# Two models in one kernel: where attention's and the state model's transposes, and the table functions, stand in the instruction order

## The chip, the cores and the metric

One core of a Trainium2 chip runs the whole program. The metric is the device time in microseconds (us) of one execution; lower is better. The engines that matter are TensorE (PE; its weight loads are shown as PEld), VectorE (DVE), ScalarE (ACT), GpSimd (POOL) and SyncE (SP), which issues nearly all transfers. Each engine works its own instructions strictly in the order in which they stand; between engines they wait for each other by semaphores.

## The reference

```python
# A: dilated local attention, x (1, 2048, 448), 16 heads of 28, window of 8 keys, 2 apart
qkv = x @ wqkv                                    # -> q, k, v
logits[s, w] = q[s] . k[s - 2*w] * 28**-0.5       # masked where s - 2*w < 0
o = softmax(logits, over w) @ v[s - 2*w]
a = o @ wo
# B: state model, x (1, 2048, 448), 448 complex states
Lam_bar = exp(dt * Lam);  B_bar = ((Lam_bar - 1) / Lam)[:, None] * Bmat
Bu = x @ B_bar.T
h[t] = Lam_bar * h[t-1] + Bu[t]
y = 2 * real(h @ Cmat.T) + x * Dskip
out = concatenate([a, b], axis=-1)                # (1, 2048, 896)
```

## The kernel before

All data fit in SBUF. For attention, the 2048 positions lie as 128 partitions by 16 slots `j`. The kernel computes, in this order on PE:

- **Transposes of attention's x** (`g_xta(jp)`, line 298): eight transposes by PE for a pair of slots, and one DVE copy of the pair from PSUM to `xTA` (L305). Pairs 7 to 0 hold slots 15 to 0.
- **Projections** (`proj(t, j)`, line 309): four matmuls of a slot with the weights of key (t=1), query (t=0) or value (t=2) (L312), then an ACT copy out of PSUM (L316). Key slots 15 to 6 come first, then queries 15 to 8, keys 5 to 0, values 15 to 0 and queries 7 to 0.
- **State model's preparation**: `b_weights(t)` (L327, seven products of B with the small matrices `G`, copied by ACT into `BT`, L329), and `b_x(j)` (L337, transposes of the state model's x for j = 0 to 7, copied into `xT`, by DVE for even j, L339, by ACT for odd j, L342).
- **The state model**, in two halves of its 448 complex states (four and three groups of 64): `ssm_in(half, j)` for j = 0 to 7 (L372, L378, ACT copy L379), a scan over the 256 chunks (`scan_mul` L387 and L388 on DVE, `scan_pe` L397 and L398 on PE, the scan itself L406 on DVE, `scan_mul` and `scan_pe` again, ACT copy L413), `ssm_mix` (L420, L422), and `ssm_out` (L432, L434, ACT copy L436, one output transfer each). Half 1's `ssm_in` stands on PE behind half 0's first `scan_pe`. The four transposes of C (`c_weights`, L352, DVE copy L354) stand between.
- **Attention's sum over values** (`av`, L537): PE adds up products `attn * v` that DVE makes one by one (`pv_mul`, L520), and `wo_j` (L554) multiplies by `wo`.

Beside this DVE carries the logits: two halves of the slots, four pieces each, every piece being one product of queries and keys (`mul`, L457), two additions (`half` L460, `quarter` L463), and, after every second piece, `rest` (L466, L467, L469); then the softmax (L485 to L496). The first piece needs queries 8 to 15 and keys from slot 6 up; the third and later pieces also need the keys' halo, rows of neighbouring partitions that SP copies from SBUF to SBUF (`halo`, L566, L567).

The order on DVE comes from a small planner at build time. `add(cost, fn)` queues a piece of DVE work with a cost in us. Two running sums are kept, the planned time of PE (`load[0]`) and of DVE (`load[1]`). Each PE step calls `pe(cost)`, which raises the first and calls `pump()`; `pump` writes queued pieces into the program for as long as DVE's sum is below PE's sum plus `lead`. `need` writes out a piece that must now be there. DVE copies of transposes and the state model's own DVE work are written where the main program calls them, so they land between queued pieces.

`tables()` (line 288) is such a piece: three DVE instructions (L289, L291, L292), and it leaves six ACT functions (L294 to L296: sine, absolute value, sine, for two slices) in a list `acts`. `proj` takes one of them out behind every second projection, as soon as the list has any:

```python
        ACT.copy(dst, src)
        count[2] += 1
        if acts and count[2] % 2 == 0:
            acts.pop(0)()
        pe(0.76)
```

All PSUM tiles come from one pool of eight banks.

Of the kernel before, what the change touches and what calls it, by code (L numbers as in the profile page):

```python
# [36 lines left out]
def kernel(  # L37
# [29 lines left out]
    def bank(dt=F32):  # L67
        return psum.tile([128, 512 if dt == F32 else 1024], dt, tag="b", name="b")
# [88 lines left out]
    acts = []  # L157
    count = [0, 0, 0]
    load = [6.0, 6.0]

    def add(cost, fn, ok=None):
        todo.append((cost, fn, ok))
        return todo[-1]

    def pop():
        c, fn, _ = todo.pop(0)
        fn()
        load[1] += c

    def pump(lead=0.0):  # L170
        while todo and load[1] < load[0] + lead and (todo[0][2] is None or todo[0][2]()):
            pop()
# [4 lines left out]

    def pe(cost):
        load[0] += cost
        pump()  # L180

    def dve(cost):
        load[1] = max(load[1], load[0]) + cost
# [115 lines left out]
    def g_xta(jp):  # L299
        tp = bank(BF16)  # L300
        tpv = tp[0:KT].rearrange("p (k j n) -> p k j n", k=4, j=2)
        for kt in range(4):
            for jj in range(2):
                PE.transpose(tpv[:, kt, jj, :], xnA[:, 2 * jp + jj, KT * kt:KT * (kt + 1)], ident[:])  # L304
        V.tensor_copy(xTA[:, :, 2 * jp:2 * jp + 2, :], tpv)  # L305
        dve(0.69)
        load[0] += 0.45

    def proj(t, j):
        ps = bank()  # L310
        for kt in range(4):
            PE.matmul(ps[:, 0:D], xTA[:, kt, j, :], wts[:, t, kt, :], start=(kt == 0), stop=(kt == 3))  # L312
        src = ps[:, 0:D].rearrange("p (h d) -> p d h", h=H)
        dst = (q_s[:, :, j * H:(j + 1) * H] if t == 0 else
               k_s[:, :, HALO + j, :] if t == 1 else v_s[:, HALO + j])
        ACT.copy(dst, src)  # L316
        count[2] += 1
        if acts and count[2] % 2 == 0:
            acts.pop(0)()
        pe(0.76)  # L320


    def b_weights(t):
        ps = bank()
        for kt in range(4):
            for i in range(2):
                PE.matmul(ps[0:KT, 128 * kt:128 * (kt + 1)], Bn[:, t, KT * kt:KT * (kt + 1)], G[:, i, t, :],  # L327
                          start=(kt == 0 and i == 0), stop=(kt == 3 and i == 1))
        ACT.copy(BT[:, :, t, :], ps[0:KT].rearrange("p (k n) -> p k n", k=4))  # L329
        pe(0.45)  # L330

    def b_x(j):
        tp = bank(BF16)
        tpv = tp[0:KT].rearrange("p (k c n) -> p k c n", k=4, c=2)
        for kt in range(4):
            for c in range(2):
                PE.transpose(tpv[:, kt, c, :], xnB[:, c, j, KT * kt:KT * (kt + 1)], ident[:])  # L337
        if j % 2 == 0:
            V.tensor_copy(xT[:, :, j, :], tp[0:KT].rearrange("p (k n) -> p k n", k=4))  # L339
            dve(0.69)  # L340
        else:
            ACT.copy(xT[:, :, j, :], tp[0:KT].rearrange("p (k n) -> p k n", k=4))  # L342
        load[0] += 0.45
# [21 lines left out]
    def ssm_in(hf, j):  # L365
        banks = []
        for pr_ in pairs(halves[hf]):
            ps = bank()
            banks.append(ps)
            for i, t in enumerate(pr_):  # L370
                for kt in range(4):
                    PE.matmul(ps[:, i * NC:(i + 1) * NC], BT[:, kt, t, :], xT[:, kt, j, :],  # L372
                              start=(kt == 0 and i == 0), stop=(kt == 3 and j == 0 and i == len(pr_) - 1))
        for ps, pr_ in zip(banks, pairs(halves[hf])):
            n = len(pr_)
            if j > 0:
                for i, t in enumerate(pr_):
                    PE.matmul(ps[:, i * NC:(i + 1) * NC], R[:, 0, t, :], Z[:, t, j - 1, :], start=False, stop=(i == n - 1))  # L378
            ACT.copy(Z[:, pr_[0]:pr_[0] + n, j, :], ps[:, 0:n * NC].rearrange("p (t c) -> p t c", t=n))  # L379
        pe(0.54 * len(halves[hf]))  # L380
# [192 lines left out]
    add(2.5, params3)  # L573
    has_R = [add(0.5, lambda: build_R(0))]
    has_G = add(1.0, build_G)
    for jp in (6, 5, 4, 3):
        proj(1, 2 * jp + 3)
        proj(1, 2 * jp + 2)
        g_xta(jp)
    proj(1, 7)  # L580
    g_xta(2)
    proj(1, 6)
    has_tab = add(6.2, tables)
    has_D = add(0.6, build_D)
    proj(0, 15)
    g_xta(1)
# [11 lines left out]
    need(has_G)  # L598
    for j in range(15, -1, -1):
        proj(2, j)  # L600
        if j % 2 == 0 and j < 14:
            b_weights(j // 2)
    for k in range(1, T - 1):
        has_R.append(add(0.6, lambda k=k: build_R(k)))
    halo(lambda lo, hi, a_, b_: v_s[lo:hi, a_:b_])
    for j in range(7, -1, -1):
        proj(0, j)
        b_x(j)
    for n_, g in enumerate((0, 1, 2, 3)):
        logits(0, n_, g)  # L610
    sm1, sm0 = softmax(1), softmax(0)
# [94 lines left out]
```

## Time and profile before

| what | value |
|---|---|
| runs shown | 182.07 us median of 3 (181.9 to 185.15) |
| the profiled execution's own time | 184.28 us |
| its span, first to last instruction | 182.5 us |
| mean granted clock of TensorE | 0.972 |
| PE busy | 167.1 us (92%) |
| DVE busy | 146.9 us (80%) |
| ACT busy | 95.2 us (52%) |
| chain that ended last | PE 58%, DVE 32%, ACT 7% |

Times in the views are microseconds from the span's start. Busy time says how long an engine worked on instructions, not that the work was on the chain that sets the end. A line of the waits view names who waited, for whom, the total in us, the number of times and the longest. A line of the timeline gives start, length, engine, source line, operation, operands, and in brackets the idle time ahead of it and what ended that.

### The profile page before, as it was taken

The numbers are of one execution on the slowest core, as the hardware profiler recorded it, in microseconds if no ns is written. First come the engines' busy times: TensorE is split into PE (matmuls) and PEld (weight loads), VectorE is DVE, ScalarE is ACT, GpSimd is POOL, SyncE is SP. The second block draws the span as 40 slices with busy tenths as digits, with TensorE's granted clock in tenths as the row PEclk, the third lists the DMA queues.
The fourth block names the chain that finished last, engine by engine and source line by source line (L and its number), as shares of the span: only waits on it lengthen the run. The fifth ranks groups of instructions, "written<-read, shape, count | busy, mean of one in ns | idle before, by whom it ended". The sixth has DMA issues, their size and how long they took to land.

```text
span 182.5 us, 3794 instructions
## 1 busy us (share of the span) xinstructions
PE 167.1 (92%) x1584; PEld 121.9 (67%) x1586; DVE 146.9 (80%) x179; ACT 95.2 (52%) x184; POOL 2.8 (2%) x22
## 2 busy tenths in 40 slices
PE   6776999999995699999999859999999999999992
PEld 7544655556673478887886525566658988887870
DVE  1674794999999999509999999994999999946721
ACT  2463429999874135442468843447832234426431
POOL 3000000000000000000001000000000000000000
PEclk9999999999999579999999978999999999999999
DMA  6999930187881000000000000211214101011212
GB/s 173 328 243 264 336 81 0 25 189 143 179 165 14 0 0 4 0 4 0 0 4 0 0 0 25 77 52 50 75 58 121 42 27 54 27 54 52 79 50 75
DMA packets 13279, 14.01 MB, mean 77 GB/s; under 512 B 4543, under 2 KB 12495, under 8 KB 13135
## 3 DMA queue, kind: packets, MB, share of 16 engines
q1 hardware_dynamic: 13191, 13.77, 29.2%
q8 instruction: 12, 0.20, 0.5%
q14 instruction: 5, 0.04, 0.1%
q10 hardware_dynamic: 71, 0.01, 0.0%
HBM read 6.89 MB, written 3.67 MB: 58 GB/s over the span
## 4 chain that ended last, share of the span: by engine, by line
PE 58%; DVE 32%; ACT 7%; issue 1%; POOL 0%; DVEq 0%; POOLq 0%; ACTq 0%
PE b L537 16%; PE b L432 12%; DVE u L457 11%; PE b L372 9%; PE b L554 7%; PE b L312 4%; DVE u L460 3%; DVE l L463 2%; DVE u L406 2%; DVE u L305 2%; PE b L135 2%; PE b L434 2%; PE b L378 2%; PE b L304 2%; PE b L422 2%
## 5 line engine op out<-in xcount | busy, mean ns | idle before, releaser
L312 PE MATMUL b<-wbuf,u 112*128 112x448 bf16 x192 | 40.0, 353 | 4.1 <-DVE u L305 3.8
L520 DVE TENSOR_TENSOR k_s<-u,v_s 128x1792 bf16<-128x1792 bf16 (+1 forms) x40 | 33.6, 897 | 4.8 <-PE b L537 4.8
L457 DVE TENSOR_TENSOR u<-q_s,k_s 128x7168 bf16<-128x7168 bf16 x8 | 31.1, 3886 | 2.8 <-ACT q_s L316 2.7
L372 PE MATMUL b<-xT,BT 112*128 112x256 bf16 x224 | 29.7, 290 | 3.9 <-DVE xT L339 3.8
L537 PEld LDWEIGHTS <-k_s 128*112 128x112 bf16 x512 | 30.6, 130 | 2.0
L537 PE MATMUL b<-ident,k_s 128*112 128x128 bf16 x512 | 30.9, 219 | 0.0
L312 PEld LDWEIGHTS <-u 112*128 112x128 bf16 x192 | 17.6, 97 | 18.4 <-DVE u L305 4.4
L372 PEld LDWEIGHTS <-BT 112*128 112x128 bf16 x224 | 23.1, 104 | 8.3 <-DVE xT L339 3.9
L379 ACT CAST u<-b 128x512 bf16<-128x512 f32 (+1 forms) x32 | 15.6, 535 | 23.9 <-PE b L378 15.7
L432 PE MATMUL b<-Cw,u 128*128 128x448 bf16 x112 | 24.9, 364 | 0.0
L559 ACT CAST ya<-b 128x448 bf16<-128x448 f32 x15 | 8.1, 537 | 16.8 <-PE b L554 13.4
L432 PEld LDWEIGHTS <-u 128*128 128x128 bf16 x112 | 10.9, 101 | 8.3 <-issue 1.1
L460 DVE TENSOR_TENSOR u<-u 128x3584 bf16<-128x3584 bf16 x8 | 16.2, 2022 | 0.2
L436 ACT CAST yo<-b 128x448 bf16<-128x448 f32 x16 | 8.6, 537 | 13.4 <-PE b L434 9.9
L554 PE MATMUL b<-u,q_s 112*128 112x448 bf16 x64 | 14.4, 352 | 0.0
L423 ACT CAST u<-b 128x512 bf16<-128x512 f32 (+1 forms) x28 | 13.1, 558 | 1.0 <-PE b L422 1.0
L316 ACT CAST k_s<-b 128x448 bf16<-128x448 f32 x16 | 8.1, 549 | 6.7 <-PE b L312 6.7
L547 ACT CAST q_s<-b 112x512 bf16<-112x512 f32 x14 | 7.3, 596 | 8.1 <-PE b L537 8.0
L305 DVE COPY u<-b 112x1024 bf16<-112x1024 bf16 x8 | 5.5, 690 | 6.6 <-PE b L304 6.6
L316 ACT CAST q_s<-b 128x448 bf16<-128x448 f32 x16 | 8.3, 534 | 3.5 <-PE b L312 3.5
L422 PE MATMUL b<-u,R 128*128 128x255 bf16 x49 | 9.9, 280 | 0.2 <-ACT u L413 0.2
L420 PE MATMUL b<-u,ident 128*128 128x512 bf16 (+1 forms) x28 | 10.1, 360 | 0.0
(119 smaller groups left out, 182.4 us busy)
## 6 DMA issues: line engine op xcount, KB each, us to landing
u<-in_B_x_dram SPq DMA_DIRECT2D x2, 896.0 KB, 14.8
out_dram<-yo SPq DMA_DIRECT2D x16, 112.0 KB, 1.7
out_dram<-ya SPq DMA_DIRECT2D x16, 112.0 KB, 2.3
u<-in_A_x_dram SPq DMA_DIRECT2D x3, 448.0 KB, 5.5
wbuf<-in_A_wqkv_dram SPq DMA_DIRECT2D x3, 392.0 KB
k_s<-k_s SPq DMA_DIRECT2D x1, 784.0 KB
v_s<-v_s SPq DMA_DIRECT2D x1, 784.0 KB, 5.9
k_s<-k_s SPq DMA_DIRECT2D x1, 588.0 KB
```

The costliest lines, as they stand in the source:

```text
L312: PE.matmul(ps[:, 0:D], xTA[:, kt, j, :], wts[:, t, kt, :], start=(kt == 0), stop=(kt == 3))
L316: ACT.copy(dst, src)
L372: PE.matmul(ps[:, i * NC:(i + 1) * NC], BT[:, kt, t, :], xT[:, kt, j, :], start=(kt == 0 and i == 0), stop=(kt == 3 and j == 0 and i == le ...
L379: ACT.copy(Z[:, pr_[0]:pr_[0] + n, j, :], ps[:, 0:n * NC].rearrange("p (t c) -> p t c", t=n))
L422: PE.matmul(ps[:, i * NC + 1:(i + 1) * NC], R[:, j, t, :], Z[:, t, T - 1, 0:NC - 1], start=False, stop=(i == n - 1))
L423: ACT.copy(Z[:, sl, j, :], ps[:, 0:n * NC].rearrange("p (t c) -> p t c", t=n))
L432: PE.matmul(ps[:, 0:D], Z[:, t, j, cols], Cw[:, t, :], start=(t == 0), stop=False)
L457: V.tensor_tensor(pr[:], qv, kv, ALU.mult)
L460: V.tensor_tensor(pr[:, :, 0:14, :], pr[:, :, 0:14, :], pr[:, :, 14:28, :], ALU.add)
L520: V.tensor_tensor(pv_of(i), attn[:, s, H * j0:H * (j0 + nj)].rearrange("p (j h) -> p j h", h=H) .unsqueeze(2).to_broadcast((128, nj, DH, H ...
L537: PE.matmul(acc[kt // kb][0:KT, o:o + 128], pvf[:, jj, KT * kt:KT * (kt + 1)], ident[:], start=(s == 0 and o == 0), stop=(s == W - 1 and o ...
L554: PE.matmul(ps[:, 0:D], oTs[n_ % 3][:, kt, jj, :], wo_p[:, kt, :], start=(kt == 0), stop=(kt == 3))
```

## The change

Five edits, all of them in the order of the work; no instruction is added, removed or resized.

1. Attention's transposes stand two pairs ahead of the projections that read them, not one: pair 6 is transposed before the first key projection, and pair `jp - 2` between the two key projections of pair `jp`.
2. The state model's eight `b_x` move from between queries 7 to 0 to between the value projections, `b_x(0)` behind value 15, `b_x(7)` behind value 1; the `b_weights` steps stand behind the even values (14, 12, ... 2).
3. The six table functions on ACT wait until 18 projections have been written, which is behind query 8, so the first stands behind key 4.
4. `pe` calls `pump(1.0)`: the planner lets DVE's queued pieces run up to 1.0 us ahead of PE's sum.
5. The queued cost of `tables` is 5.2, not 6.2.

```diff
     def pe(cost):
         load[0] += cost
-        pump()
+        pump(1.0)
...
-        if acts and count[2] % 2 == 0:
+        if acts and count[2] > 18 and count[2] % 2 == 0:
             acts.pop(0)()
...
-    for jp in (6, 5, 4, 3):
-        proj(1, 2 * jp + 3)
-        proj(1, 2 * jp + 2)
-        g_xta(jp)
+    g_xta(6)
+    for jp in (7, 6, 5, 4):
+        proj(1, 2 * jp + 1)
+        g_xta(jp - 2)
+        proj(1, 2 * jp)
     proj(1, 7)
-    g_xta(2)
     proj(1, 6)
-    has_tab = add(6.2, tables)
+    has_tab = add(5.2, tables)
...
     for j in range(15, -1, -1):
         proj(2, j)
-        if j % 2 == 0 and j < 14:
-            b_weights(j // 2)
+        if j % 2 == 1:
+            b_x(7 - j // 2)
+        elif j > 0:
+            b_weights(j // 2 - 1)
...
     for j in range(7, -1, -1):
         proj(0, j)
-        b_x(j)
```

In the built program this gives the following order on DVE. The copies of pairs 1 and 0 stand behind the three table instructions; the four `xT` copies stand among the first three logits pieces (before among the third and fourth); and ahead of half 0's first `scan_mul` there stand one `quarter` and one `mul` more than before (`mul`, `half`, `quarter`, `mul` in place of `mul`, `half`). Half 1's scan (L406) no longer has a `mul` between it and the `scan_mul` ahead of it. On SP the order of transfers is the same but for the four loads of `wo`, which stand behind the 13th and not the 14th output transfer of the state model.

## The prediction

> **What bounds it.** First the waits of PE and DVE, since these two hold the chain that ended last.
>
> ```profile
> PE b L312 <- DVE u L305: 3.8, 5, 0.8
> PE b L372 <- DVE xT L339: 3.8, 1, 3.8
> PE b L397 <- DVE wbuf L387: 2.3, 2, 2.1
> DVE u L305 <- PE b L304: 6.6, 5, 2.7
> DVE wbuf L387 <- ACT u L379: 6.4, 1, 6.4
> DVE u L457 <- ACT q_s L316: 2.7, 1, 2.7
> ```
>
> The two take turns. PE waits five times for the copy of a transposed pair, once for the last xT copy, and at the scans; DVE waits for transposes, for late queries, and for half 0 to be done. Then the timeline shows where each wait stands.
>
> ```profile
> 9.38 1.69 PE L312 MATMUL b<-wbuf,u 112*128 112x448 bf16 x8 [0.79 <-DVE u L305]
> ...
> 22.54 12.27 PE L312 MATMUL b<-wbuf,u 112*128 112x448 bf16 x64
> ...
> 30.14 0.96 ACT L316 CAST q_s<-b 128x448 bf16<-128x448 f32 x2
> ...
> 31.14 3.89 DVE L457 TENSOR_TENSOR u<-q_s,k_s 128x7168 bf16<-128x7168 bf16 x1 [2.66 <-ACT q_s L316]
> ...
> 60.90 6.42 PE L372 MATMUL b<-xT,BT 112*128 112x256 bf16 x32 [3.76 <-DVE xT L339]
> ...
> 67.60 1.91 PE L372 MATMUL b<-xT,BT 112*128 112x256 bf16 x16
> ...
> 73.39 2.03 DVE L460 TENSOR_TENSOR u<-u 128x3584 bf16<-128x3584 bf16 x1
> ...
> 81.81 0.69 DVE L387 TENSOR_TENSOR wbuf<-u,tab 128x1024 bf16<-128x1024 bf16 x1 [6.39 <-ACT u L379]
> ...
> 106.47 0.39 PE L397 MATMUL b<-wbuf,ident 128*128 128x512 bf16 x1 [2.08 <-DVE wbuf L387]
> ...
> 108.85 2.53 PE L432 MATMUL b<-Cw,u 128*128 128x448 bf16 x7
> ...
> 111.42 1.49 PE L432 MATMUL b<-Cw,u 128*128 128x448 bf16 x7
> ...
> 138.20 9.10 PE L537 MATMUL b<-ident,k_s 128*112 128x128 bf16 x160
> ```
>
> Query 8 is the sixth of the sixteen projections from 22.54, so PE has it at 22.54 + 6 x 0.767 = 27.1, but ACT evicts it at 30.6 to 31.1, behind table functions of 1.06 and 1.07: that is why the logits start at 31.14. From there DVE has no wait until 75.4. PE meanwhile waits for a DVE copy until 60.90, and its next 32 matmuls take 6.42; later 16 of the same matmuls take 1.75 from their start at 67.60 to that of the step behind them. From 108.85 PE runs without a gap to the end; what sets the time is when it gets there.
>
> **The head (edits 1, 3, 5).** Steps come from starts in the timeline: a projection 0.767 (1.53 for eight matmuls), a pair's transposes 0.46, a DVE copy 0.61, an eviction 0.53, after 0.16 from the last matmul. Pair 6 is transposed by 6.3 (its x is there: the transfer's last packet ends at 5.65), so key 15 starts at 6.5. Pair 5's x lands at 7.65, which costs PE 0.4 once. Then 12 projections up to query 14 (9.2) and six transposes (2.8) bring PE to 6.5 + 0.4 + 9.2 + 2.8 = 18.9, where it was 22.54 before: the 3.8 of waits go. The other loads land earlier than they are used (pairs 3 and 2 9.4, query weights 10.9, pairs 1 and 0 12.6, B's x 24.6). Six queries more end at 23.5, and with ACT free of table functions query 8 is out at 23.5 + 0.16 + 0.53 = 24.2. DVE must also be there. Before, it ended the piece ahead of the logits (L282) at 28.5, with 3.9 of waits for transposes since 5.71 (the list's 6.6 less its first 2.65): 24.6. Laid end to end in the new order I get 23.7. The copies of pairs 1 and 0, now behind the tables, end by 23.2; their first reader, key 3, comes at 25.0. So the logits start at 24.4, 6.7 earlier, DVE and PE about equal.
>
> **Logits up to the first scan (2, 4).** Before, DVE ran from 31.14 to 75.4 without a wait: 44.3. Now a quarter (1.1) and a mul (3.9) more stand ahead of scan_mul: 49.3, so it starts at 24.4 + 49.3 = 73.7. Three waits could break in. The third mul needs the keys' halo: issued when key 2 is out (34.6 before, now 27.5), its last packet ended at 46.9, 12.3 later; now 39.8, against 42.5 when DVE gets to it. The four xT copies need b_x: PE ends keys at 28.1 and works 19.0 for values (16 x 0.767), B products (7 x 0.44) and transposes (8 x 0.45); b_x(4) is ready at 39.1 and DVE wants it at 39.4. ACT in that stretch has 16 x 0.45, 7 x 0.48, 4 x 0.91 and four table functions of 0.75 to 1.05, 17.6 in all; it lags PE by up to 2.5, which the eight banks hold. Without that cover each us of lag delays DVE by as much.
>
> PE: values end at 47.1, queries 7 to 0 at 53.2. xT is complete by 46.8, so ssm_in starts at 53.2 and not 60.90, at full clock: 1.75 + 7 x 2.19 = 17.1 (before 19.8), then C's transposes 1.5 and ssm_in(1, 0) 1.3: 73.1. Here a new wait appears: scan_pe needs scan_mul, done at 74.3 and 74.9. PE is idle about 1.2 and again 0.4, ends scan_pe at 75.55 where it was 84.53: 9.0 ahead. Behind PE's wait stand the other seven ssm_in of half 1 and all that follows, so a late DVE here costs in full.
>
> **The clock.** After the 3.76 wait 32 matmuls cost 6.42 where 32 x 0.109 = 3.5 would do, a loss of 2.9; after 2.08 the first ssm_out took 2.37 from 108.85 to 111.22 where the next takes 1.33; after waits of 0.79 nothing slowed (1.69 for eight). The new wait of 1.2 (1.6 with its second part) lies between; nearer to 0.79, I take no loss, and 1.5 to 2.9 as the other end. The Trainium skill (TensorE: Matmul & The Clock Gate, What's actually happening) has the clock fall only after an idle window of about 3.4 us. The trace differs: it fell after 2.08. By the page the new wait would be safe and the sum unchanged; I don't lean on it.
>
> **The second half.** PE, from 75.55: ssm_in 8.1, scan_pe 0.87, two more ssm_in 3.28, three ssm_mix 2.6, so half 1's first scan_pe could start at 90.4. DVE, from 74.9: C's copies 2.14, scans 2.44, scan_mul 1.3, half 2.05, quarter 1.13, rest 2.33, mul 3.8, so the scan_mul for it starts at 90.1 and ends at 90.6 and 91.1: PE waits 0.3 and 0.25, as before (0.36 and 0.25), and nothing is gained. DVE then scans (1.87) as soon as PE is through, at 91.6 at the latest, instead of doing a mul of 3.9 first; the second scan_mul ends by 94.0 and 94.5, PE wants it after four ssm_mix (3.47) at 95.0: the 2.25 without PE work ahead of 106.47 go. With no pause the clock stays up: 0.6 less around the last scan_pe and ssm_mix, 1.04 less in the first ssm_out. Sum on the chain: 9.0 + 2.25 + 0.6 + 1.04 = 12.9.
>
> **The tail.** The first L537 moves from 138.20 to 125.3. DVE: logits end at 107, softmax maxima at 112.6 (5.6); ACT's exponentials stand one output earlier and are done as DVE asks (before DVE lost 2.24); 7.5 more to 120.1. The first products come 5 us before PE wants them (3.5 before), each 0.96 against PE's 0.89 to 1.27 per step, so PE stays the bound. The loads of wo, behind the 13th output on SP's queue, go out at about 121 (136.39 before), and the first L554 wants them at 147.09 - 12.9 = 134.2; SP carries nothing else that anyone waits for.
>
> Span 182.5 - 12.9 = 169.6. The profiled execution took 184.28, of which 1.8 lie around the span, and is 1.2% above the median; the saved time is the same on both, so the forecast is 182.07 - 12.9 = 169.2.
>
> **Rivals.** (1) Half a head: the logits start late because something else in the head binds, a load or DVE's chain of small parameter instructions (about 40 of 0.16 to 0.2). If only the table functions' delay goes, query 8 is out at 27.1 + 0.7 = 27.8 and DVE free at 28.5: start 28.5, 4.1 later, 173.3. For: DVE and PE are within 0.5 of each other, so neither may slip. Against: each load landed before its new use but one. (2) ACT paces the values: by busy time and not steps it needs 16 x 0.53 + 7 x 0.6 + 4 x 1.01 + 3.9 = 20.6 against 19.0; banks then hold PE back and the xT copies hold DVE: with the lag of 2.5, 1.6 to 4 lost, 170.8 to 173.2. For: b_x(4) has 0.3 of slack. Against: back to back, its steps were 0.42 to 0.48. (3) The halo: transfers from SBUF to SBUF that slow down by other traffic hold the third mul and everything behind it on DVE, xT(6) and scan_mul included. It costs 1:1 from a landing at 42.5 on: no gain is left at 42.5 + 12.9 = 55.4, 2% slower begins at 59, and a halo of 33 in place of 12.3, landing at 60.5, gives 169.2 + 18 = 187.2. For: the third mul began only 0.9 after the landing before, so the halo is the nearest thing to a bound there. Against: keys' and values' halo both took about 12, and the loads from HBM end by 26, before the new start at 27.5.
>
> **Chances.** Forecast 0.70 (167.2 to 172.1: down by the 1.6 that PE waits at 73 and by the 0.4 that pair 5 waits for its x, up by a cooled clock), rivals (1) and (2) 0.23 together, a halo (or another wait) that eats the gain to within 2% 0.04, one that turns it slower 0.03. About 2% is what a measurement of this kernel tells from none. All of the first two cases lie below 178.4. Cooled clock and rival (1) together make more than that; the range takes in the clock and half of (1), 169.2 + 2.9 + 2 = 174, and below it 167.
>
> **What would show it.** The first L457 at about 24.4 with next to no wait for ACT; no wait of L312 for L305 over 0.5; L372 starting at about 53 with no wait for L339 and 16 matmuls in 1.75 from the first; the 6.4 of L387 gone, and a wait of L397 for L387 of 1 to 2 in its place at 73; none of 2 near 95; L432's first seven as quick as the next; L537 at about 125. A first L457 after 27, or DVE idle ahead of an xT copy or the third L457, would prove the forecast wrong at that step.

## The result

| | before | after |
|---|---|---|
| median of four runs | 182.71 us (181.9 to 185.15) | 172.68 us (172.09 to 173.17) |
| the profiled execution, its time and span | 184.28, 182.5 | 172.66, 170.9 |
| mean granted clock of TensorE | 0.972 | 0.998 |

The change makes the kernel faster: ratio 0.946, 95% interval 0.940 to 0.953. The forecast was 169.2 in a range of 167 to 174, so the gain is there and the time is 3.5 above the forecast. The span fell by 11.6; the sum had said 12.9.

The page of the changed kernel, its first line and the clock by fortieths of the span:

```profile
span 170.9 us, 3793 instructions
...
PEclk9999999999999999999999999999999999999999
```

From 6.47, behind the first transposes, the clock is up until 170.3, 0.6 before the end. The waits of PE, then those of DVE ahead of the logits' products (who waits, for whom, total us, times, longest):

```profile
PE b L397 <- DVE wbuf L387: 1.6, 1, 1.6
...
PE b L304 <- DMA u<-in_A_x_dram: 0.9, 1, 0.9
PE b L422 <- ACT u L413: 0.7, 1, 0.7
PE b L398 <- DVE wbuf L388: 0.2, 1, 0.2
```

```profile
DVE u L457 <- ACT tab L294: 0.5, 1, 0.5
...
DVE u L457 <- ACT q_s L316: 0.3, 1, 0.3
```

The 3.8 of L312 for L305 and the 3.8 of L372 for L339 are gone. What is left on PE, beside a wait of 1.4 at the start that was there before, is one new wait at the scan, 1.6, one for a load, 0.9, and small ones. The timeline (start, length, engine, line, operation, and in brackets the wait ahead) shows where the marks of the forecast stand:

```profile
7.11 0.65 PE L304 MATMUL b<-ident,u 128*112 128x128 bf16 x8 [0.88 <-DMA u<-in_A_x_dram]
...
25.18 3.89 DVE L457 TENSOR_TENSOR u<-q_s,k_s 128x7168 bf16<-128x7168 bf16 x1 [0.31 <-ACT q_s L316]
...
33.24 3.89 DVE L457 TENSOR_TENSOR u<-q_s,k_s 128x7168 bf16<-128x7168 bf16 x1 [0.51 <-ACT tab L294]
...
43.63 3.89 DVE L457 TENSOR_TENSOR u<-q_s,k_s 128x7168 bf16<-128x7168 bf16 x1
...
53.87 3.66 PE L372 MATMUL b<-xT,BT 112*128 112x256 bf16 x32
...
75.58 0.38 PE L397 MATMUL b<-wbuf,ident 128*128 128x512 bf16 x1 [1.56 <-DVE wbuf L387]
...
96.12 0.38 PE L397 MATMUL b<-wbuf,ident 128*128 128x512 bf16 x1
...
98.27 1.49 PE L432 MATMUL b<-Cw,u 128*128 128x448 bf16 x7
...
126.58 3.63 PE L537 MATMUL b<-ident,k_s 128*112 128x128 bf16 x62
```

L372's 32 matmuls take 3.66 at once (6.42 before), the second scan has no wait (2.08 before), and the first L432 is as quick as its followers (2.53 and 1.49 before). The chain's steps happened as the sum has them, each 0.7 to 1.3 later than the forecast put it.

### The profile page after: what moved, and what is told of

Same layout as the page of the kernel before. It is cut to its first block, busy times and chain, and to the rows that moved or that the text cites. A ratio compares the mean times of both kernels' runs of the same rounds, so it can differ in the third digit from the quotient of the medians.

```text
span 170.9 us, 3793 instructions
## 1 busy us (share of the span) xinstructions
PE 162.5 (95%) x1584; PEld 120.0 (70%) x1586; DVE 146.7 (86%) x179; ACT 95.7 (56%) x184; POOL 2.8 (2%) x22
## 3 DMA queue, kind: packets, MB, share of 16 engines
HBM read 6.89 MB, written 3.67 MB: 62 GB/s over the span
## 4 chain that ended last, share of the span: by engine, by line
PE 50%; DVE 34%; ACT 6%; issue 4%; DMA 3%; SPq 0%; DVEq 0%; ACTq 0%
PE b L537 17%; PE b L432 12%; DVE u L457 11%; PE b L554 7%; PE b L312 6%; DVE u L460 6%; DVE l L463 3%; DMA u<-in_A_x_dram 3%; PE b L422 2%; PE b L420 2%; DVE R L207 2%; PE b L434 2%; DVE l L466 2%; ACT k_s L316 2%; DVE u L406 1%
## 5 line engine op out<-in xcount | busy, mean ns | idle before, releaser
L312 PE MATMUL b<-wbuf,u 112*128 112x448 bf16 x192 | 40.1, 352 | 0.1
L537 PEld LDWEIGHTS <-k_s 128*112 128x112 bf16 x512 | 30.6, 130 | 2.0
L457 DVE TENSOR_TENSOR u<-q_s,k_s 128x7168 bf16<-128x7168 bf16 x8 | 31.1, 3889 | 0.9 <-ACT tab L294 0.5
L537 PE MATMUL b<-ident,k_s 128*112 128x128 bf16 x512 | 30.9, 219 | 0.0
L312 PEld LDWEIGHTS <-u 112*128 112x128 bf16 x192 | 17.7, 97 | 14.0 <-DVE u L305 0.5
L372 PE MATMUL b<-xT,BT 112*128 112x256 bf16 x224 | 26.9, 272 | 0.1
L372 PEld LDWEIGHTS <-BT 112*128 112x128 bf16 x224 | 21.7, 97 | 3.3
L432 PE MATMUL b<-Cw,u 128*128 128x448 bf16 x112 | 23.8, 352 | 0.0
L432 PEld LDWEIGHTS <-u 128*128 128x128 bf16 x112 | 10.5, 98 | 7.5
L316 ACT CAST v_s<-b 128x448 bf16<-128x448 f32 x16 | 9.2, 612 | 0.8 <-PE b L312 0.8
```

The costliest lines, as they stand in the source:

```text
L432: PE.matmul(ps[:, 0:D], Z[:, t, j, cols], Cw[:, t, :], start=(t == 0), stop=False)
L457: V.tensor_tensor(pr[:], qv, kv, ALU.mult)
L537: PE.matmul(acc[kt // kb][0:KT, o:o + 128], pvf[:, jj, KT * kt:KT * (kt + 1)], ident[:], start=(s == 0 and o == 0), stop=(s == W - 1 and o ...
```

## The experiments

Waits, spans and clocks are of the profiled execution; ratios are to the kernel before on the same chip. A span is 1.8 shorter than the time.

**One edit undone at a time.** First the look-ahead of the transposes (edit 1):

```diff
-    g_xta(6)
-    for jp in (7, 6, 5, 4):
-        proj(1, 2 * jp + 1)
-        g_xta(jp - 2)
-        proj(1, 2 * jp)
+    for jp in (6, 5, 4, 3):
+        proj(1, 2 * jp + 3)
+        proj(1, 2 * jp + 2)
+        g_xta(jp)
     proj(1, 7)
+    g_xta(2)
     proj(1, 6)
```

> The changed kernel with its first edit undone: transposes one pair ahead again, everything else as changed. Theory (the chain runs head, then logits on DVE, then the first scan, then PE to the end, so that each us by which the logits start later costs a us): PE waits again some 0.8 five times for pair copies, less the 0.9 and 0.5 it now waits for loads; query 8 leaves ACT at about 27.8 and DVE is free at 28.5 to 29.1, so the first L457 starts 3.3 to 3.9 later than its 25.2, and the span is 174.2 to 174.8 (time 176 to 176.6). Rival A (DVE has slack later on, the head does not count): span 170.9 to 171.9. Rival B (the look-ahead is worth what PE waited less the load waits, 2.4, at the end): span 173.3.

Measured: 181.74 (180.58 to 183.27), ratio 0.987 (0.978 to 0.996). That is 9.1 above the whole change (172.68) and 5 above the expectation; the profiled execution, the slowest of the four, is 7 above it. The timeline of its head:

```profile
6.82 3.17 PE L312 MATMUL b<-wbuf,u 112*128 112x448 bf16 x8 [0.58 <-DVE u L305]
...
10.80 0.22 DVE L190 TENSOR_TENSOR sn<-sn,rk 128x56 f32<-128x56 f32 x1 [1.87 <-ACT sn L201]
...
12.23 0.69 DVE L305 COPY u<-b 112x1024 bf16<-112x1024 bf16 x1
...
12.98 2.31 PE L312 MATMUL b<-wbuf,u 112*128 112x448 bf16 x8 [2.25 <-DVE u L305]
...
16.93 3.17 PE L312 MATMUL b<-wbuf,u 112*128 112x448 bf16 x8 [0.79 <-DVE u L305]
...
34.30 3.89 DVE L457 TENSOR_TENSOR u<-q_s,k_s 128x7168 bf16<-128x7168 bf16 x1 [0.73 <-ACT q_s L316]
```

Two things I had not priced. The planner's lead of 1.0 (edit 4) writes a parameter piece, which waits for ACT, ahead of the next pair's copy; DVE works in order, so PE's wait for that copy grows to 2.25 (0.8 at most in the kernel with edits 2 and 3 below, which has neither the look-ahead nor the lead). And the clock is at half until 10.48 (until 4.8 to 7.1 in every other profile here) and again from 13.89 to 20.72, behind these waits: the same eight matmuls take 3.17 and not 1.69. The logits start 9.1 later than in the changed kernel. So what edit 4 costs or brings depends on edit 1.

A third thing stands at the scan. PE waits 1.57 for half 0's scan_mul, as it does in the changed kernel (1.56), but here the clock halves behind it, from 85.57 to 88.98:

```profile
84.72 0.38 PE L397 MATMUL b<-wbuf,ident 128*128 128x512 bf16 x1 [1.57 <-DVE wbuf L387]
...
86.33 2.77 PE L372 MATMUL b<-xT,BT 112*128 112x256 bf16 x12 [0.22 <-issue]
```

The same twelve matmuls take 1.47 behind that wait in the changed kernel. So the new wait, which the forecast took to cost no clock as the likelier of its two cases, can cost it.

The table functions (edit 3):

```diff
-        if acts and count[2] > 18 and count[2] % 2 == 0:
+        if acts and count[2] % 2 == 0:
```

> The changed kernel with its third edit undone: the six table functions stand again behind every second projection from the moment the tables are there. Theory (one chain): ACT reaches the first sine behind query 13 and waits for the tables until 23.1, then has two table functions of about 1 and the evictions in turn, so query 8 is out at 26.8, the first L457 starts 1.6 later than its 25.2, and the span is 172.5 (time 174.3); ACT lags behind PE by more, which the eight banks may or may not hold. Rival A (harmless, as other work covers it): span 170.9 to 171.3. Rival B (ACT's lag fills the banks and stops PE in the value stage): span above 174.

Measured: 177.34 (176.99 to 178.05), ratio 0.963 (0.958 to 0.968); 3 us above the expected 174.3, and 4.7 above the whole change. Its timeline:

```profile
22.67 1.06 ACT L294 ACTIVATE tab<-R 128x1024 bf16<-128x1024 f32 x1 [2.89 <-DVE R L292]
...
24.47 1.07 ACT L295 ACTIVATE R<-R 128x1024 f32<-128x1024 f32 x1
...
26.27 1.18 ACT L296 ACTIVATE tab<-R,hpib 128x1024 bf16<-128x1024 f32 x1
27.32 0.98 ACT L316 CAST q_s<-b 128x448 bf16<-128x448 f32 x2
28.33 3.89 DVE L457 TENSOR_TENSOR u<-q_s,k_s 128x7168 bf16<-128x7168 bf16 x1 [3.96 <-ACT q_s L316]
```

Three table functions, not two, stand ahead of query 8, the first of them waiting 2.89 for DVE's preparation with the queries' evictions behind it. DVE waits 3.96 for query 8; the logits start 3.15 later. With them the first scan_mul is late and PE waits long for it, now long enough to cool the clock (half from 78.79 to 82.21):

```profile
PE b L397 <- DVE wbuf L387: 4.5, 1, 4.5
```

The span of 175.2 is in rival B's range, but not for its reason: PE's longest wait for an eviction by ACT is 0.3.

The state model's transposes and B products (edit 2):

```diff
-        if j % 2 == 1:
-            b_x(7 - j // 2)
-        elif j > 0:
-            b_weights(j // 2 - 1)
+        if j % 2 == 0 and j < 14:
+            b_weights(j // 2)
...
         proj(0, j)
+        b_x(j)
```

> The changed kernel with its second edit undone: the state model's transposes of x stand again between queries 7 to 0. Theory (each engine only has to be there in time): with logits 6 us earlier DVE reaches the last xT copy at 53.8, when PE ends the last transposes at 54.5, so the wait of 3.8 ahead of L372 does not come back but one of 0.8 to 1.4, the clock stays up, and the span grows by 0.5 to 1.4 (171.4 to 172.3, time 173.2 to 174.1). Rival (the move itself took the wait of 3.8 and the cooled clock of 2.9 away): 5 to 6.7 more, span 176 to 177.6.

Measured: 171.54 (171.22 to 171.82), ratio 0.931 (0.926 to 0.935), no slower than the whole change; the spans, 169.4 to 170.0, are below the expected 171.4 to 172.3. PE's waits at ssm_in and at the scan:

```profile
PE b L372 <- DVE xT L339: 1.0, 1, 1.0
...
PE b L398 <- DVE wbuf L388: 0.2, 1, 0.2
```

With the logits 6.5 earlier, the last xT copy is only 1.0 late, and it takes the place of the wait of 1.6 at the scan. Edit 2 moves a wait from one place to the other. It also brings the 0.5 that DVE waits at the second L457, which this kernel has not.

The planner (edits 4 and 5, `pump()` and 6.2 again):

> The changed kernel with edits 4 and 5 undone: the planner has no lead and the tables cost 6.2, so DVE's scan_mul of half 0 stands one quarter and one mul earlier and half 1's scan again behind a mul. Theory (DVE's order only moves the wait): no wait of PE for half 0's scan_mul (1.8 gained, scan_pe at 73.9 and not 75.6), DVE idle 2 there, but PE waits about 0.5 for half 1's first scan_mul and about 2.4 for its second one, behind the mul of 3.9; the span is 171.5 with the clock up and 173 where that wait cools it (time 173.3 to 174.8). Rival A (an earlier scan_mul is what counts): span 169.2. Rival B (the lead is worth most of the gain): span above 175.

Measured: 172.84 (171.81 to 173.88), ratio 0.938 (0.930 to 0.946). The wait ahead of the second scan is back:

```profile
PE b L397 <- DVE wbuf L387: 2.3, 2, 2.1
```

and the four executions fall into two groups: spans of 172.1 and 172.0 at a mean clock of 0.99, and 170.1 and 170.0 at 0.998 and 1.0. Both are 1 to 1.5 below what I expected. The timeline of the first, which is the profiled one:

```profile
95.83 0.39 PE L397 MATMUL b<-wbuf,ident 128*128 128x512 bf16 x1 [2.08 <-DVE wbuf L387]
...
98.03 2.82 PE L432 MATMUL b<-Cw,u 128*128 128x448 bf16 x7
...
101.01 1.51 PE L432 MATMUL b<-Cw,u 128*128 128x448 bf16 x7
```

The same wait of 2.08 cooled the clock (half from 97.62 to 101.03, 3.41 long), by the mean clocks in two executions of four. One such stretch lowers the mean clock by 0.01 and costs 2.0 of span where PE is on the chain. Without it edits 4 and 5 bring nothing that shows here.

**One or two edits alone on the kernel before.** Edit 1 alone:

> The kernel before with the first edit alone. Theory (one chain): PE reaches query 8 some 3 earlier, but DVE is done with the tables only at 23.9, and ACT then has three table functions and the evictions ahead of query 8, as in the changed kernel without its third edit (first sine to first L457 5.7 there), so the first L457 starts at 29.6, 1.5 ahead of the kernel before; PE waits longer for the last xT copy (5 in place of 3.8) and the clock cools as before. Span 180.5 to 181.5 (the kernel before: 182.5). Rival (the 3.8 of PE waits for pair copies come off the end): span 178.7.

Measured: 181.22 (180.1 to 183.48), ratio 0.989 (0.977 to 1.000). The logits start at 30.94, hardly earlier than in the kernel before: the late queries' evictions stand behind table functions as before. This profile also has a late load: PE waits 1.96 for pair 6's x, and a stretch at half clock follows (9.31 to 12.73). Two of the four spans, 178.3 and 179.2, are below the expected 180.5 to 181.5 and close to the rival's 178.7, so what edit 1 brings alone is not settled. Edits 1 and 3 together:

> The kernel before with edits 1 and 3, without the moved state-model transposes and without the planner's lead. Theory: the first L457 at 25.0, but DVE then stands ahead of PE at the xT copies and PE again behind them: L372 starts at 57.3 (53.9 in the changed kernel), the wait ahead of it is 2.8 and cools the clock in some runs, and half 1's second scan_mul waits behind a mul, 2.1, which cooled it in half the runs of the kernel without the lead. Span 174.3 with the clock up, 176 to 178 with one or two cooled windows of 2. Rival A (edits 2, 4 and 5 are worth nothing at all, since each alone could be undone for nothing): span 170 to 172. Rival B (edits 2, 4 and 5 hold half the gain): above 178.

Measured: a time of 175.26 in the profiled execution and of 179.09 to 181.31 in the three others, spans of 173.5 (clock 1.0), 177.3, 178.3 (both 0.98) and 179.5 (0.971); the spread is too wide for a ratio, and two of the spans are above the expected 178. The logits start at 25.16. Without edits 2, 4 and 5 two waits of the kernel before are there again, the first of them shorter (2.8 for 3.8):

```profile
PE b L372 <- DVE xT L339: 2.8, 1, 2.8
PE b L397 <- DVE wbuf L387: 2.3, 2, 2.1
```

In the profiled execution neither cooled the clock, and its 173.5 is 9.0 of the 11.6; in the others the mean clocks tell of two or three stretches at half clock, and 4 to 6 of the gain are gone. Edits 2 and 3 together:

> The kernel before with edits 2 and 3, the transposes one pair ahead as before and no lead. Theory: as the head of PE and DVE is that of the kernel before but for ACT, the first L457 starts at 28.5; PE ends its queries at 57.1 and goes on without a wait at full clock, scan_pe at 77.0; 4.0 behind the changed kernel without its lead (170.1 with the clock up): span 174.1, and 176 to 177 with a cooled window or a wait for the first xT copy. Then the changed kernel without its look-ahead (178.8 to 181.5) lost 5 by its first edit's absence together with the lead, not by the absence alone. Rival (the look-ahead by itself is worth 8 to 10): span 179 to 181.

Measured: 177.21 (176.87 to 179.51), ratio 0.972 (0.958 to 0.986), spans 175.1 to 177.7, all at 0.99: the logits start at 28.46, since the head's waits are there,

```profile
PE b L312 <- DVE u L305: 3.8, 5, 0.8
...
PE b L397 <- DVE wbuf L387: 2.3, 2, 2.1
```

and the clock is at half from 100.89 to 104.3 behind the second of these. Three of the four spans (175.1 to 175.6) lie between the two cases of the expectation, 174.1 and 176 to 177 with a cooled clock, and one above. This kernel and the one with edit 1 undone differ in edits 4 and 5 alone: with them, but without the look-ahead, the logits start at 34.30 and not at 28.46, and the median is 181.74 and not 177.21.

**The clock by itself.** The kernel before, with 60 idle matmuls (of the identity with itself, into a bank that nobody reads) put where PE waits 3.76 for the last xT copy. Nothing that is computed becomes ready sooner:

```diff
+    spin = bank()
+    for _ in range(60):
+        PE.matmul(spin[:, 0:128], ident[:], ident[:], start=True, stop=True)
     for j in range(T):
```

> The kernel before with 60 matmuls of the identity on itself, 128 columns each, into a bank that nobody reads, ahead of the first ssm_in, so that PE works while it waits for the last xT copy (60 x 0.056 = 3.4 of the 3.8). Theory (a wait of 3.8 halves the clock for the matmuls behind it): L372 starts at 60.9 as before, its first 32 take 3.6 and not 6.4, and the span falls by 2.8 to 179.7. Rival A (those matmuls are slow for another reason, the bank or the weights): span 182.5, or more if the spinning delays PE. Rival B (PE's clock is not on the chain there): slow matmuls gone, span 182 to 182.5.

Measured: 181.53 (180.74 to 182.04 in ten runs), ratio 0.990 (0.986 to 0.994), span 180.3 where the profiled kernel before has 182.5. Its timeline:

```profile
57.33 3.51 PE L619 MATMUL b<-ident 128*128 128x128 bf16 x60
61.26 3.67 PE L372 MATMUL b<-xT,BT 112*128 112x256 bf16 x32 [0.41 <-DVE xT L339]
```

L372 starts 0.36 later than before and is at full speed at once, 3.67 for 6.42. All ten of its runs lie in 1.3 us and at one clock (0.99); the kernel before, on the same chip, ran between 181.94 and 186.65 at 0.963 to 0.991. Its own executions at 0.991 have spans of 180.2 there, hardly longer than the 178.9 to 180.3 of this kernel: what the idle matmuls take away is the stretches at half clock that the others have.

The same with the changed kernel less edit 1: idle matmuls behind the transposes of pairs 6 to 3 (40, 14, 14, 14):

> The changed kernel without its look-ahead (178.8 to 181.5), and in its head idle matmuls of the identity behind the transposes of pairs 6 to 3 (40, 14, 14, 14), so that PE works while it waits for the pair copies. Theory (that kernel lost in two ways: with the planner's lead DVE's second piece of parameters, which waits for ACT, stands ahead of the copy of pair 6, and the waits kept PE's clock at half up to 20.7): the waits stay, the clock opens at the first windows and stays up, the first L457 starts at 30 to 31.5 (34.3 without the spinning) and the span is 175.5 to 177.5. Rival A (it is the waits alone, the clock adds nothing): span 178.5 to 181.5 as without the spinning. Rival B (the clock alone): first L457 at 28 and span 173.5 to 174.5.

Measured: 178.08 (177.96 to 178.93), ratio 0.974 (0.968 to 0.980), all four runs at clock 1.0, the profiled span 176.2. The logits start at 30.52 and not 34.30. By the medians, undoing edit 1 costs 9.1 (181.74 - 172.68); idle matmuls that compute nothing give 3.7 of it back, and the late start that is left (30.52 against 25.18, 5.3) is the rest. Not all of the earlier start is their doing: in this profile the clock opened at 5.54, ahead of the first idle matmul at 8.62.

**Two versions that go further.** In the changed kernel the four xT copies take 2.4 of DVE ahead of the scan_mul that PE waits for. So two of them go to ACT: the changed kernel with b_x between the late queries again, but in the opposite order, and only xT(0) and xT(2) copied by DVE:

```diff
-        if j % 2 == 0:
+        if j in (0, 2):
             V.tensor_copy(xT[:, :, j, :], ...
...
+        if j % 2 == 0 and j < 14:
+            b_weights(j // 2)
...
         proj(0, j)
+        b_x(7 - j)
```

> The changed kernel with the state model's transposes of x back between the late queries (as in the one without the second edit, 169.4 to 170.0), in the opposite order, so that the first ssm_in finds its xT long made, and with two of the four xT copies of DVE given to ACT, which has slack there. Theory: the wait of 1.0 ahead of the first L372 goes, DVE reaches half 0's scan_mul 1.2 earlier (72.8), before PE wants it; span 168.6 to 169.2 (time 170.4 to 171). Rival (another wait takes its place, ACT between the queries or the scan of half 1): span 169.4 to 170.4.

Measured: 171.45 (170.62 to 172.96), ratio 0.939 (0.932 to 0.946). Three of six spans are in the expected range (168.8 to 169.1), three at 170.2 to 171.1. The wait at the scan went from 1.6 to 0.3:

```profile
PE b L304 <- DMA u<-in_A_x_dram: 0.4, 1, 0.4
PE b L397 <- DVE wbuf L387: 0.3, 1, 0.3
```

Then the same with attention's x for slots 12 and 13 loaded ahead of the key weights, and slots 8 to 11 in two transfers:

```diff
     load_x(14, 16)
-    load_w(1)
     load_x(12, 14)
-    load_x(8, 12)
+    load_w(1)
+    load_x(10, 12)
+    load_x(8, 10)
```

> The kernel of the run before, with slots 12 and 13 of attention's x loaded ahead of the key weights, and slots 8 to 11 in two transfers in place of one. Theory: the transposes of pairs 6 and 5 no longer wait for their loads (1.0 to 1.4 in the changed kernel's traces), the first L457 is 0.6 to 1.0 earlier, and the span falls by as much, to 167.8 to 168.5. Rival A (DVE's chain of parameters bounds the head, the loads are hidden): unchanged, 168.6 to 169.4. Rival B (the key weights now land too late): first L312 later, span above 169.5.

Measured: 170.91 (170.58 to 171.39), ratio 0.934 (0.930 to 0.938). The best execution is no better than that of the version without it, but all six lie within 0.8. One line of this kernel is added, so its line numbers are one higher; PE's waits have no load among them, and in its place one for DVE's copy of a pair:

```profile
PE b L313 <- DVE u L306: 0.3, 1, 0.3
PE b L398 <- DVE wbuf L388: 0.3, 1, 0.3
```

The theory of this run failed: the logits start at 24.52, 0.2 and not 0.6 to 1.0 earlier than without the reordering (24.70), and the spans, 168.8 to 169.6, lie about where rival A has them, in which DVE's chain of parameters bounds the head and hides the loads.

**The changed kernel once more**, in the same comparison:

> The changed kernel once more, beside the two variants on the same chip: span 170.3 to 171.4, time 172 to 173.2; the first L457 at 24.5 to 25.3, and L397 waiting 1.2 to 1.8 for half 0's scan_mul without a cooled window behind it. If a window cools behind that wait, the span is some 1.3 to 2 longer in that execution.

Measured: 172.77 (171.47 to 175.34), ratio 0.942 (0.936 to 0.948). Every run of the version with the early loads was below every run of this one (171.39 against 171.47), if only by 0.08, so it is the fastest here. This time's profiled execution has a span of 169.7; its transposes of attention's x wait for no load, and

```profile
24.00 3.89 DVE L457 TENSOR_TENSOR u<-q_s,k_s 128x7168 bf16<-128x7168 bf16 x1 [0.31 <-ACT q_s L316]
```

the logits start 1.18 earlier than in the first profile, in the same program.

## Why the prediction came near, and where it failed

**The head (edits 1 and 3).** The step was right and short by 0.8: L457 at 25.18, forecast 24.4. The term that was mis-sized is the load wait, priced at 0.4 once for pair 5. Pair 6's x landed at 7.07 and not at 5.65, as in the profile before, so PE waited 0.88 for it and its weight loads 0.48 for pair 5: 1.36. The first eight transposes also ran at half clock (1.06 against 0.70). Both vary between executions of one program: the second profile of the changed kernel has pair 6's transposes at 5.94 without a wait, and L457 at 24.00. The forecast took one execution's arrival for a constant. Rival (1), a load that binds in the head, holds for 0.8 of its 4.1.

**Logits up to the scan.** The first scan_mul came at 74.85, 1.15 after the forecast. To the head's 0.8 came 0.5 that DVE waits ahead of the second L457, which I had not seen. In the changed kernel the trace puts it to a table function of ACT. But it is 0.50 to 0.52 in all seven profiles of kernels with edit 2 and absent from the seven without, and with edits 4 and 5 undone the same wait is put to DVE's own instruction ahead of it:

```profile
33.79 3.89 DVE L457 TENSOR_TENSOR u<-q_s,k_s 128x7168 bf16<-128x7168 bf16 x1 [0.52 <-DVE l L463]
```

So it comes with edit 2, and the table functions are not its cause; what DVE waits for there stays open. ACT did not hold the values up: no DVE wait at an xT copy, so rival (2) is out. The halo landed at about 41.1, and the third L457 started at 43.63 without a wait; rival (3) did not come. It had 2.5 to spare.

**The new wait at the scan.** Forecast 1.2 and 0.4 without cooling; measured 1.56 and 0.23, with the clock at 1.0 behind them. In both profiled executions of the changed kernel the choice of "no loss" held. Whether it always holds is open: one of four runs of the first comparison and three of six of the last have a clock of 0.99, one stretch less, at spans of 171.4 to 173.6. No profile shows where in these runs; that it can be behind this wait, the profile with edit 1 undone shows (1.57, and half clock from 85.57). That the forecast's case held in the profiles is in part luck. With that wait at 0.3 one of twelve runs has it (the two versions above together).

**The second half.** The 2.25 at the second scan went, and L432's first seven take 1.49, as forecast. ssm_mix waits 0.69 for ACT's copy (0.2 before), some 0.5 not in the sum. The first L537 came at 126.58, forecast 125.3, and PE stayed the bound to the end.

**The sum.** 12.9 forecast, 11.6 in the first profile. In the second, with loads as early as the forecast assumed, 182.5 - 169.7 = 12.8, and L537 at 125.39. The steps added up, there with some luck: the logits start 0.4 ahead of the forecast, which makes up for the 0.5 at the second L457.

**The last line of the working** is the larger error: 2.2 of the 3.5. The 12.9 was taken from a profiled execution of 184.28 but subtracted from a median of 182.07. The saved time is not "the same on both": the executions of the kernel before differ by how many stretches of half clock they have (spans of 180.1 to 180.3 at 0.991, 181.3 to 184.7 at 0.972 to 0.981, 184.9 at 0.963), and the change removes just such stretches. The profiled execution had three (59.8 to 66.6 is two, 107.5 to 111.0 one) at 0.972; the median of 182.07, a span of about 180.3, lies with those at 0.991, which is two fewer. What it did not have could not be saved. 184.28 - 12.9 = 171.4 would have been the consistent forecast; later medians of the kernel before are 184.2 to 184.4.

**What carries the gain.** By the ratios, each to the kernel before in its own comparison, the whole change takes 5.4% off in the first and 5.8% in the last. All but edit 2 takes 6.9% and all but edits 4 and 5 takes 6.2%, so each of these can be undone alone at no cost that shows, as long as the clock stays up (spans of 170.0). All but edit 3 takes 3.7%, all but edit 1 takes 1.3%, edits 2 and 3 without the rest 2.8%, and edit 1 alone 1.1%. So the whole gain needs both 1 and 3: PE's queries have to be early and ACT has to be free of table functions, or the logits start at 30.94 (1 alone), 28.46 (3 with 2), 28.33 (all but 3), 34.30 (all but 1), against 24 to 25.2. But these two are not enough. With only them, waits of 2.8 and 2.1 are left, worth 2.6 by themselves (173.5 against 170.9), and 6 to 9 in the executions with a lower clock; beside them stands either 2, or 4 and 5. That is not a sum of parts: a share for each edit cannot be given.

Not settled is why half of the runs of the first of the two further versions lie at 170.2 to 171.1, one of them at a clock of 1.0. With the loads reordered none do, which points to the arrival of the first loads, but no profile shows one of these runs.

## What to carry to other kernels

Before a saving is subtracted from a median, see whether the profiled execution is typical of it, and whether the runs differ by the very thing that the change removes. A start that two engines hold back moves all the way only when both are relieved; undo edits singly and in pairs, since an edit can be free while another covers for it. A wait of PE of 2 us is dearer than it looks: a reordering that shortens it to 1 us (edit 2 undone, runs within 0.6), or work that fills it, also takes scatter out of the runs.

## What was not expected of the hardware

- Waits of PE of 1.6 to 2.8 us cool the clock in some executions and not in others: 1.57 did with edit 1 undone, where 1.56 at the same place did not in the changed kernel; 2.08 did in two of four, by the mean clock (edits 4 and 5 undone); 2.8 and 2.1 did not in the profiled execution with edits 1 and 3, whose three others have clocks of 0.971 to 0.98. Each stretch is 3.41 long, by the trace, and costs about 2.0 where PE is on the chain. The Trainium skill (TensorE: Matmul & The Clock Gate, What's actually happening) describes a window of 3413 ns that runs freely, which agrees with the length and with the part that chance plays; it has the clock fall after at least one idle window of about 3.4 us, and here waits of 2.08 and 1.57 were enough.
- In the head with edit 1 undone, waits of 0.58, 2.25 and 0.79 between groups of eight matmuls went with a clock at half until 10.48 and for two stretches more, 13.89 to 20.72; five waits of 0.63 to 0.79 in the kernel before did not lower it.
- 60 idle matmuls, 3.5 us of work for nothing, made a kernel 1% faster, and its runs closer to each other.
- The same first load (pair 6's x) arrived at 5.65 in the kernel before and at 7.07 in the changed one, which issue it alike, and with edit 1 alone PE waited for it until 8.15.
